# Top-k attention and a mixture of experts on one core: gate logits by token, and idle turns of TensorE ahead of the slots

## The chip, the cores and the metric

The kernel runs on one core of a Trainium2 chip. A core has five engines that run side by side, each with its own queue: TensorE (PE in the profile; its weight loads are shown apart as PEld), VectorE (DVE), ScalarE (ACT), GpSimd (POOL) and SyncE (SP), which issues most of the DMAs. The metric is the device time of one execution in microseconds; before the change it was 1231.14 us, the median of three runs (1230.12 to 1232.36).

## The reference

Attention over 8 batches of 8 heads, 576 positions and 64 channels, in which each query keeps its 32 largest scores; then a mixture of 8 experts in which each token goes to the expert of its largest logit. Cut to what matters:

```python
scores = scale * np.matmul(q, k.transpose(0, 1, 3, 2))
kth = np.partition(scores, -32, axis=-1)[..., -32:-31]
scores = np.where(scores >= kth, scores, -1e9)
attn = np.exp(scores - np.max(scores, axis=-1, keepdims=True))
attn = attn / (np.sum(attn, axis=-1, keepdims=True) + 1e-09)
x = (attn @ v).transpose(0, 2, 1, 3).reshape(4608, 512)

logits = x @ w_gate                      # 512 x 8
e_idx = np.argmax(logits, axis=1)
gate_w = softmax(logits)[arange, e_idx]
eom = sigmoid(x @ w_output_gate)         # 512 x 8
for e in range(8):                       # w1: 512 x 1024, w2: 1024 x 512 for each expert
    mask = e_idx == e
    out[mask] = gate_w[mask, None] * eom[mask, e, None] * (relu(x[mask] @ w1[e]) @ w2[e])
```

All of it is computed in fp32.

## The kernel before

The 4608 tokens are 36 tiles of 128 rows (t = 0 to 35). A tile has 8 heads, taken in 4 pairs, so the main loop has 144 steps, i = 4 t + hp, and four more to drain. Work is pipelined over the steps. In step i VectorE ranks the scores of pair i, chooses the threshold of pair i - 1 and takes the maxima of the scores of pair i + 1; ACT and GpSimd mark and weight them; TensorE turns pair i - 2 (flip, three parts: 4, 1 and 4 chunks of 128 columns, each into a PSUM tile "pst" that has two buffers), computes the scores of pair i + 2, and, every second step, attends for the pairs i - 4 and i - 3 (attend). Attend leaves the attended values of two pairs in xT, which holds, when the tile is full, four chunks of 128 channels by 128 tokens, not yet divided by the softmax sums.

When a tile is complete, tile_rows(t) is called at the end of step 4 t + 6. It queues the reciprocal r of the sums on VectorE and two *side* turns, gates and then rows. A side turn rides in the one-chunk flip part (part 1): it writes the free three quarters of that PSUM tile. One is started in a step (side_start), unless a slot is pressing (pressed). So in the plain case gates runs in step 4 t + 7 and rows in step 4 t + 8. A side turn returns two functions: `copies`, which ACT runs behind its copy of the flip, and `use`, which VectorE runs at the end of the step (side_use).

- gates: for each of the four chunks of xT a product with the two gate matrices. The weights `wg` (32 columns a chunk: 16 for each half of the chunk, as its two heads have different sums) are what the array holds, xT passes; chunk k's result goes to the partitions 32 k to 32 k + 31. ACT copies the 128 x 128 result to SBUF as `lt`. Two of the chunks of xT are also transposed back to rows and kept in `xu`.
- rows: transposes `lt`, so that tokens lie on the partitions, and the other two chunks of xT. `use` multiplies the transposed products by r (tile `tl`), and queues the sum over heads (`lg`) and, for the last tile of a group, route(g). GpSimd multiplies xu by r, and SyncE stores it as x_rows.

Tiles are taken in 12 groups. route(g) fills the queue `small` with VectorE's routing work (argmax, softmax, positions), a third side turn (product, the running counts), scatters of token numbers on GpSimd, and the slot table; the queue is drained in fixed places of a step (fill), with scatters and tables limited by a budget (DMAS, MORE, FEW, MANY). Behind it, one step or more apart each: a DMA of the list (fetch_id), a gather of the rows (fetch_x), their transpose (turn), and then the slot: 128 tokens of one expert in four *heavy pieces*, two of up (L811) and two of down (L826), one a step. Weights are loaded ahead by SyncE.

LONE = 4 * 5 + 12 = 32 is the step from which slots are looked for: ahead of it, some exponentials go by another way (ACT and GpSimd, not VectorE), and in every odd step 12 idle turns follow flip part 1 (IDLE, L450: transposes of the identity into an unused tile "pm"). From LONE on a flip part 1 that carries a side turn comes behind the heavy piece. After the last step the tail runs the remaining slots, the down products in a split form (L1130), while the last group is routed.

All engines run their queues in order; the order within a step is that of the loop at L989 to L1079.

Of the kernel before, what the change touches and what calls it, by code (L numbers as in the profile page):

```python
# [10 lines left out]
F32 = mybir.dt.float32  # L11
# [4 lines left out]
AF = mybir.ActivationFunctionType  # L16
ALU = mybir.AluOpType
AX = mybir.AxisListType
# [5 lines left out]
P = 128  # L24
# [18 lines left out]
def tile_topk_attention_moe(  # L43
# [11 lines left out]
    nc = tc.nc  # L55
# [151 lines left out]
    def run(exact, stack):  # L207
# [284 lines left out]
        def tile_rows(t, g, lg, j):  # L492

            r = st.tile([P, H], F32, name="r", bufs=2)

            xu = st.tile([P, H, D], F32, name="xu", bufs=2)
            lt = st.tile([P, P], F32, name="lt")

            def back(ps, c0):

                for k in range(2):
                    nc.tensor.transpose(ps[:, 2 + k, :], XT[t][:, c0 + k, :], ident)  # L502

            def keep(ps, c0):
                nc.scalar.activation(xu[:, 2 * c0:2 * c0 + 4, :], ps[:, 2:, :].rearrange("p c (a d) -> p (c a) d", a=2),
                                     AF.Copy)

            def gates(ps):

                for k in range(NC):  # L510
                    nc.tensor.matmul(ps[k * 32:(k + 1) * 32, 1, :], wg[:, k, :], XT[t][:, k, :], start=True, stop=True)  # L511
                back(ps, 2)

                def copies():
                    nc.scalar.activation(lt, ps[:, 1, :], AF.Copy)
                    keep(ps, 2)
                return copies, lambda: None

            def rows(ps):
                nc.tensor.transpose(ps[:, 1, :], lt, ident)  # L520
                back(ps, 0)

                def scaled(hs):
                    nc.gpsimd.tensor_tensor(xu[:, hs, :], xu[:, hs, :], r[:, hs, None].to_broadcast([P, H // 2, D]),
                                            op=ALU.mult)
                    if hs.stop == H:
                        nc.sync.dma_start(x_rows[t * P:(t + 1) * P, :].rearrange("p (h d) -> p h d", h=H), xu)
                        rows_done[0] = (t + 1) * P

                def copies():  # L530
                    keep(ps, 0)
                    for hs in (slice(0, H // 2), slice(H // 2, H)):
                        later("x", 0.6, lambda hs=hs: scaled(hs), 2)

                def use():
                    tl = st.tile([P, H, 16], F32, name="tl", bufs=1)
                    nc.vector.tensor_tensor(tl, ps[:, 1, :].rearrange("p (h e) -> p h e", h=H),
                                            r[:, :, None].to_broadcast([P, H, 16]), op=ALU.mult)
                    urgent.append(lambda: nc.vector.tensor_reduce(lg[:, j, :], tl.rearrange("p h e -> p e h"),
                                                                  axis=AX.X, op=ALU.add))  # L540
                    if t == GROUPS[g][-1]:
                        urgent.append(lambda: route(g))
                return copies, use

            sm = SM.pop(t)
            urgent.append(lambda: nc.vector.tensor_scalar(r, sm, 1e-9, None, op0=ALU.add))
            urgent.append(lambda: nc.vector.reciprocal(r, r))
            side.extend([gates, rows])
# [435 lines left out]
            gmax(0, a)  # L984

        attended = []
        IDLE = 12

        for i in range(NSTEP + 4):  # L989
            t, hp = divmod(i, NHP)  # L990
# [55 lines left out]
                exps(i)  # L1046
            for f in late:
                f()
            if 1 <= i <= NSTEP:
                unveil(i - 1)  # L1050
            if i + 1 < NSTEP:
# [234 lines left out]
```

## Time and profile before

| | before |
|---|---|
| median of the runs | 1231.14 us (1230.12 to 1232.36) |
| profiled execution | 1233.59 us, span 1231.7 us |
| PE busy | 1156.5 us (94%) |
| PEld busy | 891.5 us (72%) |
| DVE busy | 1073.8 us (87%) |
| ACT busy | 947.1 us (77%) |
| POOL busy | 715.4 us (58%) |
| granted clock of TensorE, mean | 0.982 |

The profile shows one execution. Its span goes from the first to the last instruction. A row of the groups names the line, the engine, the operation, the tiles (out<-in) with their shapes and count, and behind the bar the busy time of all of them in us and the mean duration of one in ns. Matmuls are pipelined: the duration of one is a latency, and what it costs in a row of them is the distance from start to start. In the slices each digit is a fortieth of the span, in tenths; PEclk is the granted clock of TensorE in the same way.

### The profile page before, as it was taken

To read this page: it belongs to the slowest core of one execution; us is meant where nothing else is said; L and a number is where in the kernel's file an instruction comes from. 1 tells how busy PE (TensorE), PEld (TensorE's weight loads), DVE (VectorE), ACT (ScalarE), POOL (GpSimd) and SP (SyncE) were. 2 spreads that over 40 slices of the span, in tenths; PEclk is the share of its full clock that TensorE was granted. 3 is DMA by queue.
4 is the path that set the end of the run, shared out by engine and by line. 5 is a ranking of instruction groups with operands and counts; after the bars stand their busy time and mean duration, and the time that the engine had idled before them with its cause. 6 is when DMAs were issued, how large, how long until landed. Compare 5 with 4: busy or idle time off the path is not lost.

```text
span 1231.7 us, 31165 instructions
## 1 busy us (share of the span) xinstructions
PE 1156.5 (94%) x9946; PEld 891.5 (72%) x9946; DVE 1073.8 (87%) x6151; ACT 947.1 (77%) x1892; POOL 715.4 (58%) x1191
## 2 busy tenths in 40 slices
PE   5777777899999999999999999999999999999997
PEld 3555555777777777777777777777777777689997
DVE  6999999899999999999999999999999999265443
ACT  5999998888878888887887888888878887354452
POOL 6667668555546584767457575567675467233221
PEclk7999998899999999999999999999999999999999
DMA  5301245077545619287555765474455435679980
GB/s 142 72 19 36 57 157 201 23 217 256 189 162 163 186 63 356 78 253 263 180 191 179 220 222 184 171 239 171 173 200 176 166 136 197 245 287 400 406 333 21
DMA packets 113726, 227.40 MB, mean 185 GB/s; under 512 B 19206, under 2 KB 37894, under 8 KB 112528
## 3 DMA queue, kind: packets, MB, share of 16 engines
q1 hardware_dynamic: 99712, 205.61, 48.8%
q0 software_dynamic: 7552, 18.96, 4.5%
q8 instruction: 81, 1.33, 0.4%
q10 hardware_dynamic: 6288, 0.74, 0.4%
q14 instruction: 93, 0.76, 0.2%
HBM read 206.68 MB, written 20.69 MB: 185 GB/s over the span
## 4 chain that ended last, share of the span: by engine, by line
PE 65%; DVE 15%; issue 10%; POOL 7%; ACT 2%; DMA 1%; ACTq 1%; POOLq 0%
PE pm L811 17%; PE pm L826 14%; PE po L481 10%; PE ps L309 9%; PE pst L446 9%; DVE cand L336 4%; POOL w L374 3%; DVE v L391 3%; DVE ep L420 2%; DVE cand L347 2%; DVE v L344 2%; PE pm L1130 1%; PE pst L502 1%; PE pst L800 1%; PE pst L511 1%
## 5 line engine op out<-in xcount | busy, mean ns | idle before, releaser
L374 POOL TENSOR_TENSOR w<-s,marks 128x576 f32<-128x576 f32 x288 | 363.1, 1282 | 255.3 <-DVE ep L420 117.9
L336 DVE MAX8 cand<-s 128x8 f32<-128x72 f32 x2304 | 323.8, 218 | 11.0 <-ACT s L317 10.8
L811 PE MATMUL pm<-xs,w1t 128*128 128x128 f32 x2368 | 275.6, 275 | 0.0
L446 PE MATMUL pst<-ident,ep 128*128 128x128 f32 x1296 | 218.9, 285 | 58.8 <-ACT ep L436 48.5
L811 PEld LDWEIGHTS pm<-xs,w1t 128*128 128x128 f32 x2368 | 270.2, 192 | 0.7
L371 ACT ACTIVATE marks<-s,v 128x576 int8<-128x576 f32 x288 | 220.6, 770 | 59.4 <-DVE v L344 32.9
L446 PEld LDWEIGHTS pst<-ident,ep 128*128 128x128 f32 x1296 | 147.4, 142 | 130.6 <-ACT ep L436 56.2
L391 DVE MAX8 v<-w 128x8 f32<-128x576 f32 x288 | 208.3, 748 | 31.7 <-POOL w L374 30.9
L457 ACT ACTIVATE pT<-pst 128x512 f32<-128x512 f32 (+1 forms) x432 | 201.2, 487 | 39.0 <-PE pst L502 33.9
L826 PE MATMUL pm<-w2t,ht 128*128 128x512 f32 x464 | 208.8, 593 | 0.0
L420 DVE SCALAR_TENSOR_TENSOR ep<-s,kth,ep 128x576 f32<-128x576 f32 x256 | 200.4, 815 | 0.0
L317 ACT ACTIVATE s<-ps 128x1152 f32<-128x1152 f32 (+1 forms) x145 | 163.1, 1126 | 44.9 <-PE ps L309 42.6
L386 ACT ACTIVATE ep<-s,v 128x576 f32<-128x576 f32 x256 | 185.7, 771 | 0.1
L309 PE MATMUL ps<-kst,qst 64*128 64x288 f32 (+1 forms) x1280 | 180.9, 431 | 5.1 <-ACT s L317 5.1
L481 PEld LDWEIGHTS po<-pT,v 128*64 128x64 f32 x3200 | 161.9, 139 | 24.6 <-issue 23.7
L481 PE MATMUL po<-pT,v 128*64 128x128 f32 (+1 forms) x3200 | 178.9, 269 | 0.2 <-issue 0.2
L826 PEld LDWEIGHTS pm<-w2t,ht 128*128 128x128 f32 x464 | 83.6, 190 | 83.4 <-issue 83.4
L309 PEld LDWEIGHTS ps<-kst,qst 64*128 64x128 f32 (+1 forms) x1280 | 97.8, 177 | 46.5 <-issue 23.8
L344 DVE MAX8 v<-cand 128x8 f32<-128x16 f32 (+2 forms) x864 | 128.6, 189 | 0.0
L837 POOL DMA_INDIRECT out_dram<-y,idt x40 | 56.2, 1404 | 109.1 <-ACT y L833 89.1
L347 DVE MATCH_REPLACE8 cand<-v,cand 128x16 f32<-128x16 f32 (+1 forms) x576 | 95.1, 174 | 0.0
L360 POOL TENSOR_SCALAR v<-v 128x2 f32<-128x2 f32 x144 | 37.4, 260 | 86.7 <-DVE v L344 86.5
(179 smaller groups left out, 1295.5 us busy)
## 6 DMA issues: line engine op xcount, KB each, us to landing
w1t<-in_w_dram SPq DMA_DIRECT2D x37, 2048.0 KB
w2t<-in_w_dram SPq DMA_DIRECT2D x36, 2048.0 KB
x_rows<-xu SPq DMA_DIRECT2D x36, 256.0 KB
qst<-in_qa_dram SPq DMA_DIRECT2D x70, 128.0 KB
v<-in_va_dram SPq DMA_DIRECT2D x8, 1024.0 KB
w2x<-in_w_dram SPq DMA_DIRECT2D x4, 2048.0 KB
kst<-in_ka_dram SPq DMA_DIRECT2D x14, 576.0 KB
w1x<-in_w_dram SPq DMA_DIRECT2D x3, 2048.0 KB
```

Of the source, the lines that this page charges most:

```text
L309: nc.tensor.matmul(ps[qs, a, n, :288], Q[t][rows, hp, qs], K[b][rows, hp, cols], start=True, stop=True)
L336: nc.vector.max(out=c[:, 8 * g:8 * g + 8], in_=SC[i, a][:, g * GW:(g + 1) * GW])
L371: nc.scalar.activation(m.bitcast(I8).rearrange("p (s b) -> p s b", b=2)[:, :, 1], s, AF.Sign, bias=vs[:, a, PIVOT - 1:PIVOT], scale=-(1.0 ...
L374: x = nc.gpsimd.tensor_tensor(w, s, m, op=ALU.add)
L386: nc.scalar.activation(EP[i][:, a, :], SC[i, a], AF.Exp, bias=VV[i][0][:, a, 32:33], scale=SCALE)
L391: nc.vector.max(out=VV[i][0][:, a, 24:32], in_=SW[i][0][a])
L420: LAST[0] = nc.vector.scalar_tensor_tensor(e, SC.pop((i, a)), kth_col(i, a), e, op0=ALU.is_ge, op1=ALU.mult, accum_out=SM[t][:, 2 * hp + a ...
L446: nc.tensor.transpose(ps[:, c - c0, :], pt[:, c * P:(c + 1) * P], ident)
L457: nc.scalar.activation(x, ps[:, :n, :], AF.Copy)
L481: nc.tensor.matmul(po[a * 64:(a + 1) * 64, k, qs], lhs, rhs, start=half and not k and not m, stop=(c == 3 and k == 1 and m == len(TT[t]) - 1))
L811: nc.tensor.matmul(ph[:, f - f0, :], w[:, c, f * P:(f + 1) * P], XS[s][:, c, :], start=(c == 0), stop=(c == NC - 1))
L826: nc.tensor.matmul(PY[s], HT[s][:, f, :], w[:, f, :], start=(f == 0), stop=(f == NF - 1))
```

## The change

gates swaps the operands: each chunk of xT is what the array holds, and the 32 columns of gate weights pass. The result of chunk k has the tokens on the partitions and lies in the columns 32 k to 32 k + 31, which is the form that the transpose of `lt` gave before. So `lt`, its copy and its transpose are gone, and `use` (the product with r, the sum, route) moves from rows to gates. And in the steps 2 to 31 eight more idle turns are issued behind the step's scores.

```diff
-            lt = st.tile([P, P], F32, name="lt")
...
             def gates(ps):
                 for k in range(NC):
-                    nc.tensor.matmul(ps[k * 32:(k + 1) * 32, 1, :], wg[:, k, :], XT[t][:, k, :], start=True, stop=True)
+                    nc.tensor.matmul(ps[:, 1, k * 32:(k + 1) * 32], XT[t][:, k, :], wg[:, k, :], start=True, stop=True)
                 back(ps, 2)
-
-                def copies():
-                    nc.scalar.activation(lt, ps[:, 1, :], AF.Copy)
-                    keep(ps, 2)
-                return copies, lambda: None
-
-            def rows(ps):
-                nc.tensor.transpose(ps[:, 1, :], lt, ident)
-                back(ps, 0)
...
                 def use():
                     tl = st.tile([P, H, 16], F32, name="tl", bufs=1)
...
                     if t == GROUPS[g][-1]:
                         urgent.append(lambda: route(g))
-                return copies, use
+                return (lambda: keep(ps, 2)), use
+
+            def rows(ps):
+                back(ps, 0)
...
+                def copies():
+                    keep(ps, 0)
+                    for hs in (slice(0, H // 2), slice(H // 2, H)):
+                        later("x", 0.6, lambda hs=hs: scaled(hs), 2)
+                return copies, lambda: None
...
-        IDLE = 12
+        IDLE, REST = 12, 8
...
             for f in late:
                 f()
+            if 2 <= i < LONE:
+                spare = pools["p"].tile([P, 4, P], F32, name="pm")
+                for _ in range(REST):
+                    nc.tensor.transpose(spare[:, 0, :], ident, ident)
             if 1 <= i <= NSTEP:
                 unveil(i - 1)
```

More of the change, by code (lines that the diff above doesn't have):

```diff
@@ L510, in gates, with use @@
                 for k in range(NC):
-                    nc.tensor.matmul(ps[k * 32:(k + 1) * 32, 1, :], wg[:, k, :], XT[t][:, k, :], start=True, stop=True)
+                    nc.tensor.matmul(ps[:, 1, k * 32:(k + 1) * 32], XT[t][:, k, :], wg[:, k, :], start=True, stop=True)
                 back(ps, 2)
-                def copies():
-                    nc.scalar.activation(lt, ps[:, 1, :], AF.Copy)
-                    keep(ps, 2)
-                return copies, lambda: None
+                def use():
+                    tl = st.tile([P, H, 16], F32, name="tl", bufs=1)
+                    nc.vector.tensor_tensor(tl, ps[:, 1, :].rearrange("p (h e) -> p h e", h=H),
+                                            r[:, :, None].to_broadcast([P, H, 16]), op=ALU.mult)
+                    urgent.append(lambda: nc.vector.tensor_reduce(lg[:, j, :], tl.rearrange("p h e -> p e h"),
+                                                                  axis=AX.X, op=ALU.add))
+                    if t == GROUPS[g][-1]:
+                        urgent.append(lambda: route(g))
+                return (lambda: keep(ps, 2)), use
             def rows(ps):
-                nc.tensor.transpose(ps[:, 1, :], lt, ident)
                 back(ps, 0)
@@ L533, in copies @@
                         later("x", 0.6, lambda hs=hs: scaled(hs), 2)
[L535 to L542, printed above, removed]
-                return copies, use
+                return copies, lambda: None
             sm = SM.pop(t)
```

## The prediction, made before the changed kernel had run

> **What bounds the kernel now.** I read the page first: the span, the busy shares, and the forty slices.
>
> ```profile
> span 1231.7 us, 31165 instructions
> ...
> PE   5777777899999999999999999999999999999997
> ...
> PEclk7999998899999999999999999999999999999999
> ```
>
> Until about slice 7 TensorE has room; from there to the end it is full (VectorE's share is in the next view). Then I cut the run where the granted clock changes (window, its length, then busy us of PE, PEld, DVE, ACT, POOL, then the clock):
>
> ```profile
> 35.90:165.60 129.70, 97.32 (x1058) 72.45 (x1060) 127.38 (x825) 125.75 (x271) 87.34 (x114) 1.00 0.19 43
> ...
> 203.20:206.60 3.40, 0.96 (x8) 0.42 (x4) 2.08 (x10) 1.63 (x3) 3.40 (x4) 1.00 0.01 1
> 206.60:213.40 6.80, 5.97 (x47) 5.08 (x47) 5.82 (x36) 4.72 (x11) 6.39 (x10) 0.50 0.27 78
> ...
> 220.30:223.70 3.40, 1.48 (x11) 0.66 (x7) 3.23 (x25) 3.40 (x7) 2.94 (x4) 1.00 0.04 8
> 223.70:230.50 6.80, 5.18 (x26) 3.82 (x28) 6.80 (x45) 5.63 (x12) 5.08 (x9) 0.50 0.19 57
> 230.50:1080.00 849.50, 845.12 (x7392) 634.86 (x7389) 788.54 (x4692) 678.66 (x1399) 515.36 (x917) 1.00 0.57 191
> ```
>
> So there are two regimes. Up to about 200 us VectorE sets the pace (127.38 of 129.70 us) and TensorE has a quarter of the time free. From 230.5 to 1080 us TensorE is busy 845.12 of 849.50 us: whatever a step adds to or takes from TensorE there, the run gains or loses. In between the clock falls to a half twice, each time right behind a window of 3.4 us in which TensorE had little to do (0.96 and 1.48 us).
>
> **Gates: the swap of operands.** TensorE's own timeline around one gates turn (step with L511) and the rows turn after it (step with L520):
>
> ```profile
> 493.73 0.27 PE L446 MATMUL pst<-ident,ep 128*128 128x128 f32 x1
> 493.93 0.43 PE L511 MATMUL pst<-xT,wg 128*32 128x128 f32 x8
> 494.29 0.44 PE L502 MATMUL pst<-ident,xT 128*128 128x128 f32 x2
> 494.56 0.60 PE L446 MATMUL pst<-ident,ep 128*128 128x128 f32 x4
> ...
> 502.66 0.27 PE L446 MATMUL pst<-ident,ep 128*128 128x128 f32 x1
> 502.77 0.27 PE L520 MATMUL pst<-ident,lt 128*128 128x128 f32 x1
> 502.88 0.38 PE L502 MATMUL pst<-ident,xT 128*128 128x128 f32 x2
> ```
>
> From start to start, which is what a pipelined engine is charged: the gates turn takes 494.56 - 493.73 = 0.83 us, and the transpose of lt 502.88 - 502.77 = 0.11 us. The eight gate matmuls (each product is two passes) cost only 494.29 - 493.93 = 0.36 us, because each uses 32 columns of the array and the four chunks run side by side. After the change each pass loads 128 columns of xT for only 32 columns that stream, over the whole array, one after the other. No row has that shape; these come nearest:
>
> ```profile
> L511 PEld LDWEIGHTS pst<-xT,wg 128*32 128x32 f32 x288 | 6.2, 108 | 17.4 <-issue 14.4 <-ACT xT L483 2.0
> L481 PEld LDWEIGHTS po<-pT,v 128*64 128x64 f32 x3200 | 161.9, 139 | 24.6 <-issue 23.7
> L811 PEld LDWEIGHTS pm<-xs,w1t 128*128 128x128 f32 x2368 | 270.2, 192 | 0.7
> L502 PEld LDWEIGHTS pst<-ident,xT 128*128 128x128 f32 x144 | 16.3, 141 | 7.1 <-issue 7.1
> ...
> 232.92 3.57 PE pm L811 x32
> ```
>
> A load lasts 108, 139, 192 ns for 32, 64, 128 columns: about 0.88 ns a column on a fixed 80 ns, so 128 columns occupy the load path some 0.11 us. The 32 pairs of L811 take 3.57 us, 0.112 us a pair, and there the load (0.11) and the 128 streamed columns (0.107, the rest of the pitch) are equally long. With 32 columns streamed (a quarter, 0.027 us) the load remains, so I take a pitch s = 0.112 us. The turn becomes 0.11 (the transpose ahead, which hides the first load) + 7 x 0.112 + 0.06 (the shorter load of the first transpose back, 141 against 192 ns) + 0.22 (two transposes) = 1.17 us: +0.34, less 0.11 for lt's transpose, **+0.23 us for each token tile**. Tiles 6 to 34 pass where TensorE is the bound: 29 x 0.23 = **+6.6 us**. Bounds for s: 0.06 (loads as short as a transpose's) gives 29 x 7 x 0.052 = 10.6 us less; 0.14 (load and stream in series, 0.11 + 0.03) gives 5.7 us more; a whole load each, 0.192, gives 16 more.
>
> The Trainium skill (TensorE: Matmul & The Clock Gate, Part 3, "What overlaps and what doesn't") says that a weight load runs beside a matmul in flight only where their row groups differ; here all 128 rows are used by both. By that rule the pitch is the series one, and the sum 5.7 us higher. The rows of L811 speak against it: 192 ns loads every 0.112 us.
>
> ACT loses 36 copies of lt; VectorE is the bound ahead of 230 us and TensorE after it, so I count nothing. VectorE's product with r moves to the gates turn, unchanged. It sits behind ACT's copy of the same PSUM tile there, as it did in the rows turn; behind it on VectorE wait the reduction and the next step's MAX8s, and nobody on TensorE where VectorE is ahead, which is the only case in which it has to wait. I count 0, bounds 0 to +2 us. Two waits on lt's copy near the end go, 0.43 and about 0.2 us of the other:
>
> ```profile
> 1053.01 0.66 PE L446 MATMUL pst<-ident,ep 128*128 128x128 f32 x4 [0.38 <-ACT xu L505]
> ...
> 1076.28 0.33 PE L520 MATMUL pst<-ident,lt 128*128 128x128 f32 x1 [0.43 <-ACT lt L515]
> ```
>
> That is **-0.6 us**. The last routing comes out a turn sooner too, but TensorE has other slots then, so no more follows.
>
> **A step sooner.** Logits now lead to route() at the end of the gates step, 23 and not 24 for the first group. I followed the queue of small work by hand: up to eight places a step, the product of counts one side turn later, scatters one in the first step and two in the next two (budgets 1.4 and 2.6), lists, gather and turn one step apart each. Nothing in it waits for a fixed step, so the whole moves by one: the turn of the first slot goes from step 32 to 31 (the gates of tile 6 give way, since pressed() holds, to step 32), and the first heavy piece from step 33 to step 32. This is TensorE there:
>
> ```profile
> 207.84 4.54 PE L481 MATMUL po<-pT,v 128*64 128x128 f32 x40
> ...
> 220.79 0.66 PE L446 MATMUL pst<-ident,ep 128*128 128x128 f32 x4
> 223.23 0.33 PE L446 MATMUL pst<-ident,ep 128*128 128x128 f32 x1 [1.77 <-ACT ep L436]
> 225.32 1.12 PE L446 MATMUL pst<-ident,ep 128*128 128x128 f32 x4 [1.76 <-ACT pT L457]
> ...
> 227.22 2.29 PE L309 MATMUL ps<-kst,qst 64*128 64x288 f32 x8
> ...
> 236.33 0.27 PE L446 MATMUL pst<-ident,ep 128*128 128x128 f32 x1
> ...
> 237.30 1.24 PE L309 MATMUL ps<-kst,qst 64*128 64x288 f32 x8
> 238.47 0.66 PE L446 MATMUL pst<-ident,ep 128*128 128x128 f32 x4
> 238.97 3.74 PE L811 MATMUL pm<-xs,w1t 128*128 128x128 f32 x32
> ...
> 244.44 2.40 PE L481 MATMUL po<-pT,v 128*64 128x128 f32 x40
> ```
>
> By starts: scores take 238.47 - 237.30 = 1.17 us at full clock (2.29 at 227.22), attention 2.4 (the row at 244.44), flip part 0 238.97 - 238.47 = 0.5. After the change, from 220.79 on at full clock: eight idle turns 0.9 (to 221.7), part 0 0.5 (222.2), the heavy piece 3.57 (225.7; from step 32 on part 1 follows it where a side turn rides along, L1022), part 1 with the gates 1.17 (226.9), part 2 0.53, scores 1.17 (228.6), attention 2.4 (231.0), part 0 0.5 (231.5): the second piece starts there. Before, it starts at 238.97, with what lies between 236.33 and 238.97 done besides (part 1 with rows, part 2, scores, part 0: 2.64 us). So 238.97 - 231.5 - 2.64 = 4.8 us are won, and 0.34 more since the slower gates turn is in this row and in the 29 tiles: **-5.2 us**. The waits of 1.77 and 1.76 us are filled, and the doubled durations of 225 to 230 us are gone. Bounds: without a sooner start only the clock is won, about 1.5; every wait and half-clock stretch from 202 us recovered, 8.
>
> Later groups keep their distance: slots are wanted a step sooner and routed a step sooner. One wait for a gather may go, since its group is a single tile whose routing queues behind the one ahead: **-1.0 us**, bounds -3 (three more waits of that size) and +3.6 (a heavy piece's place lost again, where a group's slots come too late).
>
> ```profile
> 465.01 0.63 PE L800 MATMUL pst<-ident,xg 128*128 128x128 f32 x4 [1.01 <-DMA xg<-x_rows,idt]
> ```
>
> **Eight idle turns.** They come after the scores in steps 2 to 31, ahead of flip part 0; 0.11 us each at full clock (as lt's transpose above), 4.70 / 24 = 0.196 at half:
>
> ```profile
> 1.36 4.70 PE L953 MATMUL po<-ident 128*128 128x128 f32 x24 [1.36 <-POOL ident masks.py:199]
> 5.99 1.24 PE L309 MATMUL ps<-kst,qst 64*128 64x288 f32 x8
> ...
> 27.54 2.29 PE L309 MATMUL ps<-kst,qst 64*128 64x288 f32 x8
> ...
> PE pst L446 <- ACT ep L436: 37.5, 26, 1.7
> ```
>
> Between 36 and 200 us TensorE waits 37.5 / 26 = 1.44 us a step for ACT's exponential ahead of flip part 1. Eight turns (0.9 us) and, in a gates step, 0.34 more end inside that wait, so they cost nothing there; at half clock (1.6 us) they push part 1, and ACT's copy of it, by 0.2 us. What they bring is activity: the thin windows at 203.2 and 220.3 us would hold 1.8 and 2.4 us of 3.4 in place of 0.96 and 1.48, more than half; the stretch from 35.9 to 165.6 us, three quarters full (97.32 of 129.70), passes unthrottled. Then attention at 207.84 takes 2.4 and not 4.54 us. What is late next there is VectorE, which gets back at most the two waits that the late TensorE had passed on to it through ACT and GpSimd:
>
> ```profile
> 219.19 0.76 DVE L391 MAX8 v<-w 128x8 f32<-128x576 f32 x1 [0.77 <-POOL w L374]
> 220.44 0.76 DVE L391 MAX8 v<-w 128x8 f32<-128x576 f32 x1 [0.48 <-POOL w L374]
> ```
>
> I take **-1.0 us** of these 1.25 (bounds 0 and 1.25). At the start, the scores at 27.54 ran at half clock; fuller windows should end that one window sooner: **-0.7 us** (bounds -1.5 to +1).
>
> The Trainium skill (the same page, Part 4) says that transposes do not count as activity in the way of matmuls. Here 24 of them alone, 0.196 us each, are followed by scores at full speed (1.24 us at 5.99), so I let them count.
>
> **Sum.** +6.6 - 0.6 - 5.2 - 1.0 - 1.0 - 0.7 = -1.9 us. The profiled execution took 1233.59 us (span 1231.7 and 1.9 around it), 2.45 over the median of 1231.14; 1231.7 on its terms is **1229.2 us** for the median.
>
> **Rivals.**
> 1. *Loads and streams in series* (s = 0.14): place, the eight gate passes of each tile from step 32 on; price 5.7 us, **1235 us**, slower. The time passes 1231.14 at s = 0.121 and the 0.2% line at 0.133. Against it stands L811's pitch; for it (beside the rule above), that no pair with so short a stream is in the trace. Chance 0.16.
> 2. *Loads quicker than L811's pitch*, near the transposes' 0.06: 10.6 us less, **1219 us**. The 192 ns against 141 speak against it. 0.11.
> 3. *The sooner start is lost again* at a later group, or at once because a turn finds no room: +3.6, **1233 us**. The continuous heavy pieces make it possible, the hand-followed queue speaks against it. 0.13.
> 4. *More is won early* (the bound of 8 in place of 5.2): **1226 us**. 0.11.
> 5. *Idle turns do not hold the clock*, so that part of the change does not do what it says: the half-clock stretches stay, 5.18 busy us of the second at half speed cost 2.6, and 1.7 more are not won: **1233.6 us**. The start of the run speaks against it. 0.06.
>
> **How the numbers follow.** Forecast 0.43, its own range 1226 to 1232. A difference under 0.2% (2.5 us: 1228.7 to 1233.6) can't be told from none. The forecast gives 0.19 faster and 0.24 same; rivals 2 and 4 0.22 faster; 1 0.16 slower; 3 0.08 same and 0.05 slower; 5 0.04 same and 0.02 slower. Faster 0.41, same 0.36, slower 0.23. The range goes from 1221, which leaves out most of rival 2, to 1238, which holds rival 1.
>
> **What would show it.** The gates turn should measure 1.17 us from the last transpose ahead to flip part 2; under 0.9 means rival 2, over 1.35 rival 1. The first L811 should start near 222 us, the second piece near 231, with clock 1.00 between 203 and 232 us. TensorE should stay without idle after that; a step without a heavy piece is rival 3. I am wrong altogether if the early VectorE-bound steps grow by more than 0.1 us each.

## The result, and the profile after

The changed kernel takes **1241.57 us** (median of four runs, 1241.13 to 1242.49); the kernel before took 1231.75 us on the same chip (1230.12 to 1232.39). The ratio is **1.0083** (95%: 1.0065 to 1.0100): about 10 us slower, where 2 us faster had been forecast. The profiled execution took 1242.49 us, with a span of 1240.7. The page after:

```profile
span 1240.7 us, 31488 instructions
...
PE   5898987999999999999999999999999999999997
...
PEclk7999999999999999999999999999999999999999
```

Slices 2 to 6 look better than before (8 and 9 in PE where 7 stood), PEclk has lost its 8s, and still the span is 9 us longer. The windows of the kernel after (columns as in the prediction):

```profile
35.90:165.60 129.70, 116.82 (x1229) 93.83 (x1229) 128.57 (x827) 126.09 (x268) 87.93 (x113) 1.00 0.28 80
...
230.50:1080.00 849.50, 841.39 (x7270) 644.62 (x7269) 778.05 (x4666) 674.51 (x1357) 510.05 (x912) 1.00 0.57 189
```

Up to 165 us TensorE has the idle turns (116.82 us busy in place of 97.32), and VectorE is the bound as before. In the middle TensorE stands idle 8.1 us, where it was 4.4. The gates turn and the first slot of the kernel after, on TensorE:

```profile
485.61 0.27 PE L446 MATMUL pst<-ident,ep 128*128 128x128 f32 x1
485.72 0.98 PE L510 MATMUL pst<-wg,xT 128*128 128x32 f32 x8
486.53 0.42 PE L501 MATMUL pst<-ident,xT 128*128 128x128 f32 x2
486.78 0.60 PE L446 MATMUL pst<-ident,ep 128*128 128x128 f32 x4
```

```profile
207.15 4.07 PE L481 MATMUL po<-pT,v 128*64 128x128 f32 x40
...
219.25 1.09 PE L1046 MATMUL pm<-ident 128*128 128x128 f32 x8
...
220.62 3.74 PE L805 MATMUL pm<-xs,w1t 128*128 128x128 f32 x32
...
228.92 3.74 PE L805 MATMUL pm<-xs,w1t 128*128 128x128 f32 x32
...
1033.74 3.74 PE L805 MATMUL pm<-xs,w1t 128*128 128x128 f32 x32
```

The same places of the kernel before, the first piece of the first slot and of the 28th:

```profile
232.76 3.74 PE L811 MATMUL pm<-xs,w1t 128*128 128x128 f32 x32
238.97 3.74 PE L811 MATMUL pm<-xs,w1t 128*128 128x128 f32 x32
...
1034.14 3.74 PE L811 MATMUL pm<-xs,w1t 128*128 128x128 f32 x32
```

The gates turn takes 486.78 - 485.61 = 1.17 us, as worked out. The first slot starts 12.1 us sooner (220.62 in place of 232.76; its second piece at 228.92 in place of 238.97). But 27 slots later only 0.4 us of it are left: from the first slot to the 28th the kernel after needs 1033.74 - 220.62 = 813.1 us, the kernel before 801.4, so **11.7 us go in the middle**, and 27 times 0.23 explain only 6.2. The rest of the run takes 207.0 us after and 197.6 before; part of these 9.4 is the work beside one heavy piece, since the slots stand one step earlier among the steps.

Who waited for whom between 240 and 1040 us, on VectorE and TensorE (total us, times, longest). Before:

```profile
DVE tl L537 <- ACT xu L505: 6.5, 14, 2.1
...
PE pst L446 <- ACT pT L457: 0.8, 1, 0.8
```

After:

```profile
DVE tl L515 <- ACT xu L504: 27.2, 22, 2.7
...
PE pst L446 <- ACT pT L457: 6.5, 5, 1.9
PE pst L446 <- DVE tl L515: 0.8, 1, 0.8
```

The row of 6.5 us is five waits of TensorE for ScalarE's copy of a flip, where the kernel before has one. The longest, on ScalarE and TensorE:

```profile
655.88 2.20 ACTq L776 DMA_DIRECT2D idt<-ids  x3
...
658.19 0.78 ACT L371 ACTIVATE marks<-s,v 128x576 int8<-128x576 f32 x1 [2.69 <-DMA idt<-ids]
...
659.72 0.74 ACT L457 ACTIVATE pT<-pst 128x512 f32<-128x512 f32 x2
...
660.35 0.66 PE L446 MATMUL pst<-ident,ep 128*128 128x128 f32 x4 [1.92 <-ACT pT L457]
```

ScalarE spends 2.20 us on issuing three list fetches, its marks start late, its copy of the flip comes behind them in its queue, and TensorE waits 1.92 us for the buffer. All five such waits stand right behind a list fetch. In the tail a further wait appears, where the first slot's down products want the split that VectorE makes behind the last tile's routing:

```profile
1084.19 3.74 PE L805 MATMUL pm<-xs,w1t 128*128 128x128 f32 x32
...
1094.84 0.60 PE L1128 MATMUL pm<-w2h,htl 128*128 128x512 f32 x1 [2.12 <-DVE htl L1119]
...
1102.01 3.17 PE L805 MATMUL pm<-xs,w1t 128*128 128x128 f32 x27
```

This slot takes 1102.01 - 1084.19 = 17.8 us; in the kernel before it took 1093.58 - 1080.23 = 13.4, since the last routing ran under a heavy piece there. Both long waits, 1.92 and 2.12 us, are followed by a window at half clock (third last column):

```profile
661.70:665.10 3.40, 3.40 (x30) 2.65 (x29) 3.40 (x24) 2.91 (x6) 1.61 (x8) 0.51 1.01 400
1095.10:1098.50 3.40, 3.40 (x9) 2.63 (x9) 3.02 (x20) 0.00 (x0) 2.25 (x5) 0.50 1.05 404
```

### The profile page after: what moved, and what is told of

It is laid out like the page before. It is cut to its first block, busy times and chain, and to the rows that moved or that the text cites. A ratio compares the mean times of both kernels' runs of the same rounds, so it can differ in the third digit from the quotient of the medians.

```text
span 1240.7 us, 31488 instructions
## 1 busy us (share of the span) xinstructions
PE 1184.1 (95%) x10150; PEld 933.9 (75%) x10150; DVE 1068.7 (86%) x6151; ACT 946.9 (76%) x1856; POOL 713.3 (57%) x1191
## 4 chain that ended last, share of the span: by engine, by line
PE 63%; DVE 16%; issue 10%; POOL 7%; ACT 2%; ACTq 1%; DMA 0%; POOLq 0%
PE pm L805 15%; PE pm L820 14%; PE po L481 10%; PE ps L309 9%; PE pst L446 9%; DVE cand L336 4%; POOL w L374 3%; DVE v L391 3%; DVE ep L420 2%; DVE cand L347 2%; PE pst L510 2%; DVE v L344 2%; PE pm L1128 1%; PE pst L501 1%; PE pst L794 1%
## 5 line engine op out<-in xcount | busy, mean ns | idle before, releaser
L371 ACT ACTIVATE marks<-s,v 128x576 int8<-128x576 f32 x288 | 220.6, 769 | 60.2 <-DVE v L344 37.2
L446 PE MATMUL pst<-ident,ep 128*128 128x128 f32 x1296 | 215.2, 281 | 40.3 <-ACT ep L436 22.9
L391 DVE MAX8 v<-w 128x8 f32<-128x576 f32 x288 | 206.3, 748 | 28.5 <-POOL w L374 27.8
L457 ACT ACTIVATE pT<-pst 128x512 f32<-128x512 f32 (+1 forms) x432 | 200.5, 484 | 13.9 <-PE pst L501 12.7
```

What stands on the lines that cost most here:

```text
L371: nc.scalar.activation(m.bitcast(I8).rearrange("p (s b) -> p s b", b=2)[:, :, 1], s, AF.Sign, bias=vs[:, a, PIVOT - 1:PIVOT], scale=-(1.0 ...
L391: nc.vector.max(out=VV[i][0][:, a, 24:32], in_=SW[i][0][a])
L446: nc.tensor.transpose(ps[:, c - c0, :], pt[:, c * P:(c + 1) * P], ident)
L457: nc.scalar.activation(x, ps[:, :n, :], AF.Copy)
```

## The experiments

All ratios are to the kernel before, timed on the same chip, with the 95% interval in brackets. Differences in us are differences of ratios times 1231.7. The first theory, **A**, was read from the rows above: the longer gates turns, the list fetches and the uncovered last routing cost, and the sooner start puts the heavy pieces where fetches hurt.

### Idle turns, taken away and alone

```diff
-            if 2 <= i < LONE:
-                spare = pools["p"].tile([P, 4, P], F32, name="pm")
-                for _ in range(REST):
-                    nc.tensor.transpose(spare[:, 0, :], ident, ident)
```

> The changed kernel without its eight idle turns a step (everything else of the change stays). Theory A (the change loses by three things: the gates turns of 1.17 us instead of 0.83, new waits of TensorE behind the list fetches, and a routing that the last tile's heavy piece no longer covers; the idle turns only help): the half-clock stretches between 165 and 231 us come back and the time is 0.5 to 3 us above the changed kernel's 1241.6. Rival I (the idle turns themselves cost the time, by holding back the score turns or the copies of the early steps): 3 to 10 us below the changed kernel. Nothing of the waits after 230 us should differ by theory A beyond a shift of all of them by one amount.

Measured: 1246.54 us, 1.0109 (1.0093 to 1.0124). The same lines added to the kernel before, and nothing else:

> The kernel before with the eight idle turns and nothing else of the change. Theory A: 0.5 to 3 us below the kernel before, with no half-clock stretch between 165 and 213 us. Rival I (the idle turns cost the time): 3 to 10 us above it.

Measured: **1228.93 us, 0.9971** (0.9961 to 0.9980). The idle turns give 3.2 us in the changed kernel and 3.6 us in the kernel before. Two windows of the kernel before:

```profile
165.60:169.00 3.40, 3.40 (x36) 3.26 (x32) 3.33 (x17) 2.67 (x7) 3.40 (x3) 0.51 0.00 0
223.70:230.50 6.80, 5.18 (x26) 3.82 (x28) 6.80 (x45) 5.63 (x12) 5.08 (x9) 0.50 0.19 57
```

and with idle turns alone:

```profile
165.60:169.00 3.40, 3.40 (x42) 2.58 (x39) 3.29 (x15) 3.07 (x8) 3.40 (x4) 1.00 0.02 5
223.70:230.50 6.80, 6.80 (x77) 5.98 (x78) 6.80 (x44) 6.80 (x15) 4.08 (x6) 1.00 0.04 14
```

Rival I is out. The Trainium skill (TensorE: Matmul & The Clock Gate, Part 4) says that transposes do not count as activity in the way of matmuls; the turns here are transposes alone, and the clock column goes from 0.51 to 1.00, so the trace does not agree.

### The swap with routing not sooner

```diff
-                    if t == GROUPS[g][-1]:              # in the use of gates
-                        urgent.append(lambda: route(g))
...
+                def use():                              # the use of rows
+                    if t == GROUPS[g][-1]:
+                        urgent.append(lambda: route(g))
+                return copies, use
```

> The changed kernel, with its swapped gates operands and idle turns, but a group's routing is queued a step later, from the use of the rows as in the kernel before. Theory A: the gates turns cost 0.23 us a tile, some 6.5 us over 29 tiles, the idle turns give back 0.5 to 3, and the waits behind list fetches and the uncovered last routing are not there, since the heavy pieces fall as in the kernel before: 3 to 6 us above the kernel before (1235 to 1238). Rival S (the sooner step alone loses the time, and the longer gates turns are hidden): within 2 us of the kernel before or below it. Rival G (the gates swap alone loses all of it): 9 us or more above it.

Measured: **1248.42 us, 1.0126** (1.0111 to 1.0142), 15.5 us over the kernel before. Theory A fell here: with the heavy pieces in their old steps the loss is larger, not smaller, and the sooner step gives 5.3 us back. The swap costs some 19 us against the kernel with idle turns alone. Does a pass cost more than its 0.112 us?

```diff
+                    for _ in range(2):
                         nc.tensor.matmul(ps[:, 1, k * 32:(k + 1) * 32], XT[t][:, k, :], wg[:, k, :], start=True, stop=True)
```

> The changed kernel with each of the eight gate passes of a tile issued twice, to price a pass where it stands (the second overwrites the first, with the same result). If nothing hides them, 8 passes of 0.111 us for 29 tiles are 25.8 us: theory A expects 21 to 28 us above the changed kernel. Rival S (the gates turn is hidden beside other work): under 12 us.

Measured: 1273.35 us, 1.0325 (1.0310 to 1.0341), 29.8 us over the changed kernel by the ratios. On its timeline the sixteen passes of one tile are

```profile
498.27 1.87 PE L511 MATMUL pst<-wg,xT 128*128 128x32 f32 x16
```

1.87 us in place of 0.98, which is 0.111 us for each of the eight added, 25.8 us for 29 tiles. The passes lie open, at the price worked out; the other 4 us were not followed. That leaves some 12 us of the swap's 19 that are no passes.

### VectorE's part, in its old and its new place

The changed kernel moves VectorE's product with r (`tl`) and its sum (`lg`) from the end of the rows' step to the end of the gates' step. The prediction had this at nothing. **Theory D** puts the rest of the loss there. First, the swap without that move:

```diff
+                def copies():                           # gates, swapped operands
+                    nc.scalar.activation(lt, ps[:, 1, :], AF.Copy)
+                    keep(ps, 2)
+                return copies, lambda: None
...
+                    nc.vector.tensor_tensor(tl, lt...   # in the use of rows
```

> The kernel before with the eight idle turns and the swapped operands, and nothing sooner: ScalarE still copies the gates' output to a tile in SBUF, and VectorE scales it and sums it in the use of the rows, a step later, as in the kernel before (only the transposition by TensorE is gone). The kernel with idle turns alone is 2.8 us below the kernel before, and the swap with VectorE's part at the end of the gates' own step was 15.7 us above it. Theory D (the longer gates turns cost their 0.23 us a tile, some 6.5 us, and the rest of that difference, some 12 us, is VectorE's 0.66 us of scaling and summing, which at the end of the gates' step falls ahead of the short step that VectorE bounds): 2 to 6 us above the kernel before, 1234 to 1238. Rival G (the swapped passes themselves cause the rest, through the waits of the flips behind them): 12 us or more above it.

Measured: **1233.66 us, 1.0018** (1.0009 to 1.0027). The swap itself costs 5.8 us over the kernel with idle turns alone, and Rival G is out. Then the reverse: old operands, and VectorE's two instructions issued once more for each tile, into tiles that nobody reads, at the end of the gates' step,

```diff
+                    nc.vector.tensor_tensor(tx, lt..., r..., op=ALU.mult)
+                    urgent.append(lambda: nc.vector.tensor_reduce(lx, tx..., op=ALU.add))
```

> The kernel before with the eight idle turns, old operands, and VectorE's scaling and summing done once more per tile into tiles that nobody reads, at the end of the gates' own step. It adds 0.66 us of VectorE a tile, 24 us in all, in the place to which the change moved it. Theory D: 7 to 14 us above the kernel with idle turns alone (1228.9), 1236 to 1243. Rival G (VectorE's place does not matter, the swapped passes do): within 3 us of it.

Measured: **1241.57 us, 1.0080** (1.0064 to 1.0095). And the same two instructions at the end of the rows' step:

> The same added work of VectorE, 0.66 us a tile, but at the end of the rows' step, where the kernel before has its own and where the longer step follows. Theory D: 0 to 5 us above the kernel with idle turns alone, and clearly less than where it stands at the end of the gates' step. Rival (VectorE's total counts, not the place): as much as there.

Measured: **1231.44 us, 1.0000** (0.9991 to 1.0010). The same 0.66 us a tile costs 13.4 us in the one place and 3.6 us in the other. Not all of that difference lies in the middle. In the profiled runs the first slot starts at 234.2 us and at 228.9, and from the first slot to the 28th they need 808.1 and 802.5 us. So 5.3 us are lost ahead of the first slot (the first run has half-clock windows at 210.7 and 227.8 us there, the second has none) and 5.6 us in the middle. The runs also differ in a second thing: at the end of the gates' step the added product must wait for ScalarE's copy of this step, at the end of the rows' step it reads a copy that is a step old.

One reading of the loss in the middle starts from the steps. Starts of the steps' scores in the kernel before, with the gates and the rows turn between them:

```profile
584.15 1.24 PE L309 MATMUL ps<-kst,qst 64*128 64x288 f32 x8
...
592.80 1.24 PE L309 MATMUL ps<-kst,qst 64*128 64x288 f32 x8
598.68 1.24 PE L309 MATMUL ps<-kst,qst 64*128 64x288 f32 x8
...
606.31 0.43 PE L511 MATMUL pst<-xT,wg 128*32 128x128 f32 x8
607.47 1.24 PE L309 MATMUL ps<-kst,qst 64*128 64x288 f32 x8
612.68 0.27 PE L520 MATMUL pst<-ident,lt 128*128 128x128 f32 x1
613.54 0.76 PE L309 MATMUL ps<-kst,qst 64*128 64x288 f32 x4
```

and the busy time of the engines in 800 us of its middle (PE, PEld, DVE):

```profile
240.00:1040.00 800.00, 796.42 (x6981) 597.38 (x6979) 765.76 (x4572) 653.47 (x1341) 500.18 (x893) 1.00 0.57 191
```

TensorE's steps are 8.65, 5.88, 8.79 and 6.07 us long; the long ones hold the attention. VectorE is busy 765.76 of 800 us, so a step of 29.4 / 4 = 7.35 us has about 7.0 us of VectorE's work, if every step has the same. By this estimate VectorE falls some 1 us behind TensorE in a short step, and in a long one it gets ahead again. In the middle the gates turn ends a **long** step for most tiles. An instruction of VectorE that must wait there for this step's gates and for ScalarE's copy would hold VectorE, whose queue is in order, until TensorE's long step is over, and take away the lead that the short step uses up. At the end of the rows' step, a short one, VectorE would be behind anyway and seldom have to wait. The waits of VectorE between 240 and 1040 us, where `tl` stands behind the gates' step (swap, routing not sooner):

```profile
DVE tl L515 <- ACT xu L504: 17.6, 12, 2.3
```

With the swap and `tl` in its old place no such row is left. Two readings remained: TensorE may lose its time because VectorE now has to read the PSUM buffer of the flips before it is free, or because VectorE itself stands still. To tell them apart, ScalarE copies the gates' output to SBUF, VectorE reads the copy, still in the gates' step:

```diff
+                def copies():
+                    nc.scalar.activation(lt, ps[:, 1, :], AF.Copy)
+                    keep(ps, 2)
...
-                    nc.vector.tensor_tensor(tl, ps[:, 1, :]...
+                    nc.vector.tensor_tensor(tl, lt...
```

> The variant with swapped operands, idle turns, VectorE's part at the end of the gates' step and routing not sooner (1248.4 us), but ScalarE copies the gates' output to a tile in SBUF ahead of its copy of the rows, and VectorE reads that. It frees the PSUM buffer of the flips without VectorE; VectorE still waits, at the end of the gates' step, for TensorE and for one copy of ScalarE. Against the variant with the same copy and VectorE's part a step later (1233.7 us) only the place differs. Theory H (half and half: TensorE's waits for VectorE to have read the PSUM buffer are one part, VectorE's own standing still at that place the other): 1237 to 1244. Theory V (VectorE's standing still is all of it): 1245 to 1249. Theory P (the held buffer is all of it): 1232 to 1236.

Measured: **1250.84 us, 1.0159** (1.0146 to 1.0173). The buffer is free early and the time is not better but 4.1 us worse. Against the same copy with VectorE's part a step later only the place differs, and with it how fresh the copy is; that is 17.4 us. (In the profiled runs 12.7 of it lie between the first slot and the 28th. The 4.1 us against the swap with routing not sooner lie ahead of the first slot, 233.9 against 229.7 us; the middle is 2.6 us shorter.) Its waits on VectorE, and then on TensorE:

```profile
DVE tl L516 <- ACT lt L522: 15.8, 12, 2.2
```

```profile
PE pst L510 <- ACT xT L483: 4.9, 4, 1.8
PE pst L446 <- ACT pT L457: 3.6, 9, 1.7
```

VectorE stands still nearly as long as before, and TensorE's waits move to copies of ScalarE. So the held buffer is not what costs most of the time: of the three theories V comes nearest, whose 1245 to 1249 the run passes by 1.8 us.

But that VectorE's standing still is what costs is not shown, and two traces speak against it. Both runs come in the next section. The first is the swap with routing not sooner and the list fetch on SyncE, where TensorE waits seven times for `tl`:

```profile
PE pst L446 <- DVE tl L515: 8.6, 7, 1.8
...
580.69 0.27 DVE L515 TENSOR_TENSOR tl<-pst,r 128x128 f32<-128x128 f32 x1
...
581.02 0.66 PE L446 MATMUL pst<-ident,ep 128*128 128x128 f32 x4 [1.51 <-DVE tl L515]
```

In all seven, as here, VectorE had not waited ahead of `tl`: it came there late, and TensorE's next flip had to wait for it. In the tiles in which VectorE did stand still for `tl` (16.3 us in all), TensorE did not wait for `tl`. The second is the changed kernel with the list fetch on SyncE, with `tl` at the end of the gates' step for every tile:

```profile
DVE tl L515 <- ACT xu L504: 22.8, 19, 2.2
...
240.00:1040.00 800.00, 799.15 (x6953) 613.67 (x6950) 756.80 (x4555) 652.24 (x1310) 492.87 (x889) 1.00 0.57 189
```

VectorE stands still longer there than in any run of this section, and TensorE is busy 799.15 of 800 us. What is shown, then: with routing in its old step, the place of VectorE's part is worth 13 to 17 us. Where TensorE waits for `tl`, VectorE is late at the end of the gates' step. Why it is late in those tiles and not in the others was not followed.

### List fetches

In the changed kernel TensorE's waits stood behind list fetches. The fetch on another queue:

```diff
-                ov = nc.values_load(row, engines=[ACT], ...
+                ov = nc.values_load(row, engines=[SP], ...
-            nc.scalar.dma_start(it, ids[place, :])
+            nc.sync.dma_start(it, ids[place, :])
```

> The changed kernel with the fetch of a slot's list (its read of the row number and the transfer of the ids) issued by SyncE and not by ScalarE. Theory A: ScalarE no longer spends 2.1 us on each issue, the five waits of TensorE for a copy of the flips right behind such a fetch (at 507, 567, 658, 721 and 900 us, 7.4 us together) and the half-clock stretch at 662 us go: 3 to 7 us below the changed kernel. Rival W (these waits come from ScalarE's whole load between two heavy pieces, and the fetch is only where they show): within 1.5 us of the changed kernel, with waits for the same copies elsewhere.

Measured: **1233.05 us, 1.0009** (0.9998 to 1.0019): 9.1 us of the 10.2 are gone. TensorE's waits between 240 and 1040 us shrink to one row,

```profile
PE pst L446 <- DVE tl L515: 0.3, 1, 0.3
```

and the half clock at 662 us is gone. The same in the kernel before with idle turns, with and without the earlier split of the next part, and in the swap with routing not sooner:

> The kernel before with the eight idle turns and the list fetch on SyncE, nothing else. Theory L: with VectorE's part in its old place there is slack under most fetches, so the move gives 0 to 2 us: 1227 to 1229. Rival (a fetch on ScalarE costs in any case what it cost in the changed kernel, 8.5 us): 1220 to 1222.

Measured: 1228.22 us, 0.9976 (0.9962 to 0.9990).

> The kernel before (its old gates turn, its old step) with the eight idle turns, the list fetch on SyncE and the earlier split of the first tail slot. Theory A: the kernel before has fewer of these waits, so the fetch and the split give less here, 0 to 3 us, and the idle turns 0.5 to 3: 1 to 5 us below the kernel before, 1226.5 to 1230.5. Rival W: the fetch's move gives nothing here either, and the time is within 2 us of the kernel before with idle turns alone.

Measured: 1229.66 us, 0.9986 (0.9976 to 0.9995).

> Swapped operands, VectorE's part at the end of the gates' step, routing not sooner, idle turns (the variant that took 1248.4 us), and now the list fetch on SyncE. Theory L (VectorE's moved 0.66 us only takes the slack; what spills to TensorE is ScalarE's list fetch of 2.1 us on top of it): 6 us or more below that variant, 1237 to 1242. Rival D (the moved work costs its 13 us by itself): within 3 us of it, 1245 to 1249.

Measured: 1246.40 us, 1.0126 (1.0112 to 1.0141). So the fetch costs nothing in the kernel before and nothing in the swap with routing not sooner, where VectorE's place costs its 13 us without it (Theory L is out there); in the changed kernel it costs 9 us. What is shown: of the three the fetch is dear only in the changed kernel, and the sooner routing is a condition, since VectorE's part has the same place in the swap with routing not sooner. Whether that place is a second condition stays open; no run had the sooner routing without VectorE's part being moved in any tile, as the one needs the other.

The other side of it is as large. With the fetch on SyncE, the sooner routing gives 14.4 us (1.0126 to 1.0009), where it gives 5.3 with the fetch on ScalarE. That is about what VectorE's place had cost. In the profiled runs the middle of the changed kernel with the fetch on SyncE takes 804.0 us, and that of the swap with VectorE's part in its old place 804.3 (with the fetch on ScalarE; no run had that swap with it on SyncE). So the 13 us are a price of the place together with the late routing, not of the place alone; by which wait the two are tied was not followed. The Trainium skill (DMA: Bandwidth & Descriptors, Issuing engine by pattern) gives simple loads to SyncE; here that is worth 9.1 us in one kernel and nothing measurable in two others.

### The tail

The split of the first tail slot's second weight, issued ahead of the last routing:

```diff
+        for part in range(2):
+            splitted(cur[0], part)
         background()
```

> The changed kernel with one thing moved: the two parts of the split of the first tail slot's second weight are issued on ScalarE and VectorE ahead of the last tile's routing, not behind it. Theory A: the wait of 2.12 us ahead of the first tail slot's down pass and the half-clock stretch at 1095 us go, or shrink, and the second tail slot starts 2 to 4.5 us sooner: 2 to 4.5 us below the changed kernel. Rival T (the tail's first slot waits for the routing's own lists or for its ids, whatever the order of the split): within 1 us of the changed kernel.

Measured: 1243.00 us, 1.0092 (1.0077 to 1.0108): nothing won. Its wait is another one, and longer:

```profile
PE pst L578 <- ACT ex L565: 4.7, 1, 4.7
```

This wait is for the routing's own exponential. Split and routing share ScalarE and VectorE, and in both orders the second of them was waited for.

> The changed kernel with both the earlier split of the first tail slot and the list fetch on SyncE. Theory A: the two gains add, 5 to 11 us below the changed kernel, 1231 to 1236. If either rival T or W holds, only the other's gain is seen.

Measured: 1234.23 us, 1.0025 (1.0014 to 1.0035): the fetch's gain alone. Then the first tail slot without a split, on top of the list fetch on SyncE:

```diff
+                    if s == plain:
+                        up(s, f0)()          # and down(s, 4 * part) below
```

> The changed kernel with the list fetch on SyncE (1233.05 us), and in the tail the first slot computed as in the middle, with its weights whole and not split into two parts. Theory T (the tail's first slot loses 3 to 4.5 us since its split shares ScalarE and VectorE with the last routing): its down pass costs 1.6 us more by itself and waits for no split, so the second tail slot starts 1 to 3 us sooner: 1230 to 1232. Rival (the wait only moves to the next slot's split or to the lists): 1233 to 1236.

Measured: **1230.01 us, 0.9985** (0.9976 to 0.9994), 3.0 us less, uncertain by some 2 us. So about 3 us of the tail's loss hung on the split of this slot beside the last routing.

### The sooner step for some tiles only

Swap and sooner routing for the first group alone, the old gates turn for all others (idle turns, list fetch on SyncE):

```diff
+                if g == 0:
+                    for k in range(NC):
+                        nc.tensor.matmul(ps[:, 1, k * 32:(k + 1) * 32], XT[t][:, k, :], wg[:, k, :], ...
```

> The change made for the first group's tiles alone (swapped operands, logits and routing a step sooner), the old gates turn and the old step for all others, with the eight idle turns and the list fetch on SyncE. Theory D: the first slot starts near 220 us as in the changed kernel (some 8 us sooner in equal work), the middle goes at the old pitch of 29.4 us a tile, and the last routing is uncovered as in the changed kernel (4 to 5 us lost): 4 to 9 us below the kernel before, 1223 to 1228, below both kernels. Rival (the sooner start is lost whatever the pitch): within 2 us of the kernel before with idle turns alone, 1227 to 1231.

Measured: 1239.89 us, 1.0066 (1.0053 to 1.0080), a miss. One slot ends and the next begins:

```profile
391.41 3.60 PE L833 MATMUL pm<-w2t,ht 128*128 128x512 f32 x8
412.62 1.56 PE L818 MATMUL pm<-xs,w1t 128*128 128x128 f32 x8
```

Between 395 and 412 us no heavy piece is there to run: the second group comes out a step late for slots that stand a step earlier, and what the start won is lost at once. So every group has to be sooner. That needs the move in the **last tile of each group** only, 12 of 36 (8 gate passes each, 96 in the trace):

```diff
-                if g == 0:
+                if t == GROUPS[g][-1]:
```

> The change made for the last tile of each group alone (11 of 36: swapped operands, logits and routing a step sooner), the old gates turn and the old place of VectorE's part for the other 25; idle turns, list fetch on SyncE. If the parts are independent: -3.6 us for the idle turns, -5 for the sooner step, +2 for 9 longer gates turns where TensorE is the bound, 0 to +5 for VectorE's part moved in 11 tiles, +0 to -2 for the fetch: 1224 to 1231. The hole of 14 us that the first group alone being sooner left ahead of the second group's first slot should not be there. Rival (the sooner step's loss at the tail and in the middle eats its gain whatever the pitch): 1231 to 1237.

Measured: 1228.52 us, 0.9974 (0.9965 to 0.9983). With the first tail slot whole as well:

> The change for the last tile of each group alone with idle turns and list fetch on SyncE (1228.5 us), and the tail's first slot computed whole. There the first tail slot took 17.7 us where the kernel with idle turns alone has 13.3; a whole first slot gave back 3.0 us in the changed kernel with the list fetch on SyncE. Expected: 3 to 4 us less, 1224 to 1226, below both kernels. Rival (the tail's wait is another here): 1227.5 to 1229.

Measured: **1226.26 us, 0.9956** (0.9943 to 0.9970), the fastest of all, 5.4 us below the kernel before and 15.6 below the changed one. It is only 1.8 us below the kernel with idle turns alone (0.9971), and without the whole tail slot (0.9974) it gained nothing over that kernel: most of what is won comes from the idle turns.

## Why the prediction was wrong

| step | predicted | measured |
|---|---|---|
| idle turns | -1.7 us | -3.6 in the kernel before, -3.2 in the changed one |
| swap of operands, VectorE's part in its old place | +6.0 (6.6 - 0.6) | +5.8 |
| VectorE's part moved to the gates' step | 0, bounds 0 to +2 | +13.3 |
| routing a step sooner, with later groups | -6.2 (5.2 + 1.0) | -5.3 |
| sum | -1.9 | +10.2 |

The measured column adds one edit at a time in this order (0.9971, 1.0018, 1.0126, 1.0083); each difference is uncertain by some 2 us. The last row depends on where the fetch is issued: with the fetch on SyncE in both of its runs it is -14.4.

Where the time lies, in the profiled runs (start of the first slot; from there to the start of the 28th, 108 steps in each; the rest of the span; us):

| kernel | first slot | to the 28th | rest |
|---|---|---|---|
| idle turns alone | 228.6 | 801.5 | 198.3 |
| and the swap, VectorE's part in its old place | 229.5 | 804.3 | 197.7 |
| and VectorE's part in the gates' step | 229.7 | 819.6 | 197.4 |
| and routing sooner (the changed kernel) | 220.6 | 813.1 | 207.0 |
| and the list fetch on SyncE | 219.9 | 804.0 | 206.3 |

Sooner routing starts the first slot 9.1 us sooner and makes the rest 9.6 us longer (a part of both is one step of other work that changes sides). What it wins lies in the middle.

**The step that failed**, in the order of the first table, is the sentence on VectorE: "It sits behind ACT's copy of the same PSUM tile there, as it did in the rows turn; behind it on VectorE wait the reduction and the next step's MAX8s, and nobody on TensorE where VectorE is ahead, which is the only case in which it has to wait. I count 0, bounds 0 to +2 us." It measured +13.3 us, with routing in its old step. The sentence looks at one case only, VectorE ahead and waiting, and for that case the traces bear it out: behind such a wait TensorE did not wait for `tl`. The case that it leaves out is VectorE coming late to `tl`; then TensorE's next flip waits for VectorE, seven times and 8.6 us in all in the run shown above. The added work (13.4 against 3.6 us) and the copy in SBUF (17.4 us) show that the place counts, together with how fresh the copy is that is read there; how all of the 13 us reach TensorE stays open. The prediction's own row for 230 to 1080 us held a hint, 788.54 us of VectorE in 849.50, so VectorE could be late. A high share alone does not decide: in the changed kernel with the fetch on SyncE it is busy 756.80 of 800 us, and TensorE loses nothing.

**Seen from the changed kernel**, where the parts meet, the split is another: idle turns -3.2, swap near +6, list fetches +9.1, tail about +3, which leaves about -4.7 for the sooner routing and VectorE's part together. So a second step failed, and in this kernel it is the larger one: the prediction let the lists move along without a price ("Nothing in it waits for a fixed step, so the whole moves by one"), and it had no term for what their issue does to ScalarE and TensorE in the new step. Moving the fetches off ScalarE takes 9.1 of the 10.2 us away. For the tail it said: "The last routing comes out a turn sooner too, but TensorE has other slots then, so no more follows." It has, but their split waits for the same VectorE and ScalarE: 2.12 us of wait and a half clock.

**Gates passes.** Right: 1.17 us a turn in the trace, pitch 0.111 by the doubled passes, the sum right within its uncertainty (in the profiled runs the middle grows by only 2.8 us with the swap). Rivals 1 and 2 fall. The rule of the Trainium skill that the prediction weighed (TensorE: Matmul & The Clock Gate, Part 3, "What overlaps and what doesn't") would have a load wait for the stream ahead of it; sixteen passes with 192 ns loads in 1.87 us do not agree.

**A step sooner.** Right in kind: the first heavy piece came one step sooner. Its start was put near 222 us and came at 220.62, the second near 231 and came at 228.92; that the step gave 5.3 us of the 6.2 forecast is luck, since what the sooner start won came back at the end and the gain was made in the middle, where only 1.0 had been forecast. "Later groups keep their distance" holds: the first pieces go on every four steps. Rival 3 (a sooner start lost at a later group) happened only where the first group alone was sooner.

**Idle turns.** The turns do hold the clock in most places (rival 5 falls), and the size was halved: the term took the start and the stretches near 206 and 223 us, and those at 165.6 and 186.1 us, which the turns also lift, had no price. Two things in it were too hopeful. The stretch near 206 us mostly stayed: with idle turns alone the clock is 0.50 from 205.2 to 212.0 us, and in the changed kernel the attention at 207 us still took 4.07 and not 2.4 us. And near 224 us the clock is not held every time: four of the other runs with the same turns have a half-clock window that begins between 223.9 and 227.8 us.

**The signs named for being wrong** were not the right ones: the early VectorE-bound steps did not grow. The failure was in the middle, where VectorE and ScalarE were not looked at.

## What to carry to other kernels

Before you move an instruction up, ask whether its engine comes to the new place late, and which engine waits for it then; that it has nothing to do but wait when it comes early is no answer. A change that moves one thing a step sooner also moves what hangs on it, here the list fetches, so look at the engine that issues them too. Prices of this kind do not add: here one place cost 13 us with late routing, and nothing in the middle with sooner routing and the fetch on another queue. And where only the last item of a group is wanted sooner, move only that one.

## What the runs showed of the hardware that was not expected

A wait of TensorE far shorter than a window of 3.4 us, in an otherwise full stretch, can be followed by a window at half clock: in the changed kernel the waits of 1.92 us ahead of 660 us and of 2.12 us ahead of 1095 us were each followed by 3.4 us at 0.51 and 0.50. Behind the four shorter waits for the same copies, up to 1.65 us, the clock stayed full. The length alone does not decide: in the swap with routing not sooner a wait of 1.40 us ahead of 578.5 us was followed by 3.4 us at 0.51, and in the kernel before with idle turns and the list fetch on SyncE a wait of 2.18 us ahead of 461.8 us was followed by 3.4 us at 1.00.

Three list fetches hold ScalarE's queue for 2.20 us, 0.73 us each, more than one of its copies takes (0.36 to 0.60 us on average).
